# Turning float64 weight words into float32: four VectorE operations in place of three and one on GpSimd

## The chip, the cores and the metric

The kernel runs on 1 core of one Trainium2 chip. The metric is the device time of one execution in microseconds, the median of several runs. A profile records one further execution; its own time is the span from its first to its last instruction.

## The reference

The inputs are q, k and v (8 batches, 8 heads, 576 positions, 64 per head) and three weight matrices. Keys and values are averaged over groups of 8 positions, which leaves 72 of each. Then comes softmax attention against the 72, and a gated layer on the result:

```
k_p = k.reshape(B, H, Sp, 8, D).mean(axis=3);  v_p likewise      # Sp = 72
scores = matmul(q, k_p^T) / sqrt(D);  attn = softmax(scores)
x = matmul(attn, v_p) as [4608, 512]
out = ((x @ w_a) * (x @ w_b)) @ w_out            # w_a, w_b [512, 1536], w_out [1536, 512]
```

The weights arrive as float64, since they are scaled by a float64 number. The kernel reads them as pairs of 32-bit words and turns each pair into one float32 on the chip. The host only changes the layout.

## The kernel before

**Split products.** Every operand of a TensorE product is split into a high part (a rounded copy, made by ScalarE) and a low part (the difference, made by `low_part`, L171), and three products are summed in place of one.

**Tiles and steps.** The 4608 rows are worked in 9 tiles of 512. A tile takes 12 steps, one for each 128 of the 1536 inner columns. A step makes `a` (L552 to L554, PSUM tile psa), copies it to SBUF (L557), makes `b` (psb), multiplies both (L530), splits the product (hh L533, hl L171), and adds the product of the step before with w_out to `acc` (L573 to L575). For each step `split_weight` splits a block of each of the three weight matrices again (L238 on ScalarE: jha, jhb, jho; L171 on GpSimd: jla, jlb, jlo).

**Attention.** The queries come in 40 chunks (`chunk`): their scores (psc, L392), the scores less their maximum (L376, L377), exp (L426), the sum (z, L428 to L430), the division (s, L432), the split (pr, rem), the transposition (ptr L477, p L478) and the product with the values (po, L510 to L513, then xh and xl). Chunks of the first tile are done before the first step; those of a later tile run among the steps of the tile before it. `load_keys` and `load_values` average the keys and values (kp, vp, vwide, vdiag).

**Conversion.** `convert_weights(name, j, first)` is a generator for each of the matrices a, b and o. For each of 12 blocks of 128 x 512 it loads 1024 words per partition into its part of the tile `words` (one buffer for each matrix, L201), makes `low` (the low word by 2 to the power of -29, L211) and `mag` (the absolute value of the high word read as float32, L212) on ScalarE, then works on VectorE (L213, L216, L222) and ends with an addition on GpSimd (L226). Each converted block stays in SBUF for all 9 tiles, so the 36 conversions are done once, in the early part of the run.

**Order.** The order of each engine's instructions is written out by the program (`manual_schedule`). Each piece of work is a generator of class `Chains`; `yield n` puts its next part n slots later, and six slots make a step. Within a slot the ranks are: products, splits, chunks, weights, keys. From the third block on, a conversion waits until the step two before its own has begun, plus 0, 2 or 4 slots for a, b and o. Each engine works through its own instructions strictly in that order, and so does the queue of the DMA issues on SP.

Of the kernel before, what the change touches and what calls it, by code (L numbers as in the profile page):

```python
# [9 lines left out]
F32 = mybir.dt.float32  # L10
# [3 lines left out]
AF = mybir.ActivationFunctionType  # L14
ALU = mybir.AluOpType
# [10 lines left out]
NF = DF // P  # L26
NK = DM // P
# the high word of float64 2**-126, read as float32
MIN_HIGH = 2.0**-15 * 1.125
SCALE = 1.0 / float(D) ** 0.5  # L30
# [10 lines left out]

# of the pooled keys the first KM are multiplied with the values head pair by head pair, the KR
# that remain for four heads at a time: (hi, lo, hi) x 4 heads x KR rows
KM = D
KR = SP - KM
NR = 3 * 4 * KR
NG = H // 4
# a step of the inner loop takes this many slots of TensorE's time, a tile NF steps
SLOTS = 6
TILE_SLOTS = SLOTS * NF  # L50
# queries whose products with the values are made together: of the first two tiles, of the others
BLOCK, BLOCK_LATER = 256, 384
# tiles that hold something for a short time only
NTMP = 6
# chunks whose scores' three parts are summed in PSUM (the others' by VectorE)
SUMMED = 9
# steps by which the weights' conversion keeps ahead of the products, in the first tile
AHEAD = 2
# groups of TensorE's work in a slot in which the inner loop waits
GROUPS = 4  # L60
# slots: when a step's weights are split; between the parts of a chunk; what a chunk takes, and
# those of the second tile one after the other; how early a batch's keys and values come
SPLIT_A, SPLIT_B, SPLIT_O = 1, 4, 4
PROBS_GAP, VALUE_GAP = 2, 4
CHUNK, CHUNK_LATER, CHUNK_GAP = 34, 32, 10
KEYS_AHEAD, VALUES_AFTER = 18, 16
# the same before the first step: chunks one after the other, the values, the second batch's keys,
# the weights' loads and how much later their conversion begins
EARLY_GAP, VALUES_START, KEYS_START, WEIGHTS_START, CONVERT_AFTER = 1, 2, 4, 10, 5


class Chains:
    """Chains of work (generators), resumed slot by slot: a chain yields how many slots its next part
    comes later, or PE to get TensorE between two groups of the inner loop's products. done holds
    what has been issued."""

    PE = "PE"
# [36 lines left out]
def attn_moe_kernel(ctx: ExitStack, tc: tile.TileContext, q, k, v, vr, wa, wb, wo, out):  # L114
    nc = tc.nc
# [4 lines left out]
    PE = Chains.PE  # L120
    mark, wait, done = chains.mark, chains.wait, chains.done
    PRODUCTS, SPLITS, CHUNKS, WEIGHTS, KEYS = ((x, 0) for x in range(5))

    def tmp(name, dtype=F32):
        return sb.tile([P, 512], dtype, tag="tmp", name=name, bufs=NTMP)
# [5 lines left out]
    w_dram = {"a": wa, "b": wb, "o": wo}  # L131
    # pooled keys, heads in pairs on the diagonal: [(h%2, d), h//2, hi/lo, h%2, key]
    kdiag = [const.tile([P, NK, 2, 2, SP], F32R, name=f"kdiag{i}") for i in range(2)]
    # pooled values, heads in pairs on the diagonal: [(h%2, key), h//2, hi/lo, (h%2, d)]
    vdiag = [const.tile([P, NK, 2, P], F32R, name=f"vdiag{i}") for i in range(2)]
    # row (part, h%4, key) belongs to which of four heads
    mask = const.tile([P, 4], F32, name="mask")
    # where the weights' bits arrive: later the place of the blocks' transposed probabilities
    work = sb.tile([P, 2 * NK * BLOCK_LATER], I32, tag="work", name="words", bufs=1)
# [4 lines left out]
    early = sum(t == 0 for t in tile_of)  # L144
    # chunks of a batch and a tile whose products with the values are made together
    blocks, start = [], 0

    def cut(chunks, limit):
        """the cheapest blocks: a product takes its columns' time, or that of its weights' load"""
        best = None  # L150
        for x in range(1, len(chunks) + 1):
            total = sum(flat[c][2] for c in chunks[:x])
            if total > limit:
                break
            cost, rest = cut(chunks[x:], limit) if x < len(chunks) else (0, [])
            cost += max(total, 2 * P)
            if best is None or cost < best[0]:
                best = cost, [chunks[:x]] + rest
        return best
# [8 lines left out]
    vrems, parts, xtiles, turned, begun = {}, {}, {}, {}, []  # L168
# [3 lines left out]

    # the first batch's inputs wait where the last weights come later
    early_q = raw["a"][:, NF - early:, :].rearrange("p c (g s) -> p c g s", g=NK)
# [20 lines left out]
    def convert_weights(name, j, first):  # L195
        """float64 bits to the nearest float32: the sign and the exponent's top bit stay, 27 bits of
        the high word move up by three, what lies below float32's normal range becomes zero, and
        the low word rounds into the last three bits"""

        def load_words(f):  # L200
            nc.sync.dma_start(area[name], w_dram[name][:, f, :].bitcast(I32))  # L201

        load_words(0)
        yield first
        for f in range(NF):
            words = area[name].rearrange("p (c w) -> p c w", w=2)
            hi, lo = words[:, :, 1], words[:, :, 0]
            w = raw[name][:, f, :]
            wi = w.bitcast(I32)
            low, mag = tmp(f"wlow_{name}{f}", I32), tmp(f"wmag_{name}{f}")  # L210
            nc.scalar.activation(low, lo.bitcast(U32), AF.Copy, scale=2.0**-29)  # L211
            nc.scalar.activation(mag, hi.bitcast(F32), AF.Abs)  # L212
            nc.vector.tensor_scalar(  # L213
                out=wi, in0=hi, scalar1=0x07FFFFFF, scalar2=3, op0=ALU.bitwise_and, op1=ALU.logical_shift_left
            )
            nc.vector.scalar_tensor_tensor(  # L216
                out=wi, in0=hi, scalar=-(1 << 30), in1=wi, op0=ALU.bitwise_and, op1=ALU.bitwise_or
            )
            if f + 1 < NF:
                load_words(f + 1)  # L220
            yield 1
            nc.vector.scalar_tensor_tensor(  # L222
                out=w, in0=mag, scalar=MIN_HIGH, in1=w, op0=ALU.is_ge, op1=ALU.mult
            )
            yield 1
            nc.gpsimd.tensor_tensor(out=wi, in0=wi, in1=low, op=ALU.add)  # L226
            mark("weight", name, f)
            yield 2
            # not far ahead of the products, and not all three matrices at once
            while f + 1 >= AHEAD and (len(begun) <= f + 1 - AHEAD or chains.now < begun[f + 1 - AHEAD] + 2 * j):  # L230
                yield 1
# [52 lines left out]
    def load_values(b):  # L284
# [4 lines left out]
        for x0 in range(0, NK + NG, 2):  # L289
# [12 lines left out]
            for j in range(2):  # L302
                x, rows = x0 + j, P if x0 < NK else NR
                vv = vraw[j][:rows].rearrange("p (d j) -> p d j", j=POOL)
                if b == 0 and 0 < x < NK:
                    for n in (4, 2, 1):
                        to = vp[:rows, x].unsqueeze(2) if n == 1 else vv[:, :, :n]
# [5 lines left out]
        for e in range(2):  # L313
            r = slice(e * KM, e * KM + KM)
            nc.scalar.mul(vd[r, :, 0, r], vp[r, :NK], 1.0 / POOL)
        # each row's values at its head's place, zero at the others'
        wide = tmp(f"vwide_{b}").rearrange("p (r j e d) -> p r (j e) d", r=NG, j=2, e=2)
        for r in range(NG):
            nc.vector.scalar_tensor_tensor(
                out=wide[:NR, r],  # L320
                in0=vp[:NR, NK + r].unsqueeze(1).broadcast_to([NR, 4, D]),
                scalar=1.0 / POOL,
                in1=mask[:NR].unsqueeze(2).broadcast_to([NR, 4, D]),
                op0=ALU.mult,
                op1=ALU.mult,
# [5 lines left out]
        for e in range(2):  # L331
            r = slice(e * KM, e * KM + KM)
            nc.vector.scalar_tensor_tensor(
                out=vd[r, :, 1, r],
                in0=vp[r, :NK],
                scalar=1.0 / POOL,
                in1=vd[r, :, 0, r].bitcast(F32),
                op0=ALU.mult,
                op1=ALU.subtract,
# [8 lines left out]
    def chunk(i):  # L348
        b, o, n = flat[i]
        t, col = divmod(b * S + o, NT)  # L350
        first = i < early
# [14 lines left out]

        # scores less their maximum
        kd = kdiag[b % 2]
        s = sb.tile([P, H, SP], F32, tag="s", name=f"s_{i}")
        m = sb.tile([P, H], F32, tag="m", name=f"m_{i}")  # L370
# [52 lines left out]

        # probabilities
        yield 1
# [9 lines left out]
        yield 1  # L435
        # split, the keys that remain apart: [of four heads, (hi, lo, hi), h%4, key]
        yield from wait(("turned", i - 2))
# [11 lines left out]

        # transposed, and a block's products with the values  # L450
        j = block_of[i]
# [132 lines left out]
    def have(t):  # L584
        """all chunks of a tile are done"""
        return all(("value", block_of[i]) in done for i in range(len(flat)) if tile_of[i] == t)

    with tc.manual_schedule():
# [18 lines left out]

        # later chunks end in even steps, the first of them after what it takes to get there
        tail = [i for i in range(early, len(flat)) if tile_of[i] == 1]
# [76 lines left out]
```

## Time and profile before

| what | value |
| --- | --- |
| median of 3 runs | 1107.91 us (1107.82 to 1108.48) |
| span of the profiled execution | 1107.4 us |
| TensorE busy | 1038.7 us, 94% |
| VectorE (DVE) busy | 611.5 us, 55% |
| ScalarE (ACT) busy | 522.9 us, 47% |
| GpSimd (POOL) busy | 618.8 us, 56% |
| mean granted TensorE clock | 0.981 |

Busy time is the union of an engine's instructions. An instruction's recorded duration holds also the time in which it had been started and could not go on, so an operation of one shape can show quite different durations. The profile's 40 slices of 27.7 us show TensorE at 90% or more from the ninth slice on, and VectorE at 90% or more from the second to the eighth.

### The profile page before, as it was taken

Reading aid. Unit: us, or ns where it says so; the run is one execution under the profiler, and the core shown is the slowest. Engines: PE = TensorE matmul, PEld = TensorE weight load, DVE = VectorE, ACT = ScalarE, POOL = GpSimd, SP = SyncE. Lnnn points to the kernel's source line nnn. Section 1 sums busy time; section 2 is a strip of 40 time slices with the busy share of each in tenths; the row PEclk is TensorE's granted clock in tenths of the full one; section 3 lists DMA queues with packets and bytes.
Section 4 is the critical chain, followed back from the end, with each engine's and each line's share of the span. In section 5 each row is a group of like instructions: output and inputs, shape, how many; then the busy total and the mean of one; then the engine's idle time right before and its main releaser. Section 6 shows DMA issues by size and latency. Waiting matters only on the chain.

```text
span 1107.4 us, 13650 instructions
## 1 busy us (share of the span) xinstructions
PE 1038.7 (94%) x4964; PEld 861.7 (78%) x4964; DVE 611.5 (55%) x917; ACT 522.9 (47%) x1051; POOL 618.8 (56%) x501
## 2 busy tenths in 40 slices
PE   4378887899999999999999999999999999999998
PEld 4356665688887888888888888888888888888887
DVE  7999999863348333753367335654458343332212
ACT  3655555544445445544455445444445444443332
POOL 6557776655555555555555455554556455554442
PEclk9989888999999999999999999999999999999999
DMA  6454344120023000400021002200211020001001
GB/s 220 128 154 126 105 145 131 48 89 1 1 71 110 1 1 22 148 3 1 1 94 59 1 1 91 82 1 1 69 55 49 1 67 1 1 1 38 1 1 38
DMA packets 29874, 59.59 MB, mean 54 GB/s; under 512 B 7120, under 2 KB 7120, under 8 KB 29808
## 3 DMA queue, kind: packets, MB, share of 16 engines
q1 hardware_dynamic: 29808, 58.73, 16.9%
q8 instruction: 39, 0.64, 0.3%
q14 instruction: 27, 0.22, 0.1%
HBM read 49.28 MB, written 9.44 MB: 53 GB/s over the span
## 4 chain that ended last, share of the span: by engine, by line
PE 81%; DVE 14%; issue 2%; DMA 1%; ACT 1%; POOL 0%; SPq 0%; DVEq 0%; POOLq 0%; ACTq 0%
PE acc L573 9%; PE psa L552 8%; PE psb L552 8%; PE acc L575 8%; PE acc L574 8%; PE psa L554 8%; PE psa L553 8%; PE psb L554 8%; PE psb L553 8%; PE ptr L477 2%; PE psc L406 2%; DVE wo_raw L216 1%; DVE wo_raw L213 1%; DVE wa_raw L222 1%; DVE wb_raw L216 1%
## 5 line engine op out<-in xcount | busy, mean ns | idle before, releaser
L171 POOL TENSOR_TENSOR jlb<-wb_raw,jhb 128x512 fp32r<-128x512 f32 x108 | 142.9, 1323 | 220.9 <-ACT jhb L238 220.9
L530 DVE TENSOR_TENSOR h<-psb,h 128x512 f32<-128x512 f32 x108 | 74.5, 690 | 343.6 <-PE psb L554 340.4
L171 POOL TENSOR_TENSOR jla<-wa_raw,jha 128x512 fp32r<-128x512 f32 x108 | 143.9, 1332 | 143.0 <-ACT jha L238 117.5
L557 ACT COPY h<-psa 128x512 f32<-128x512 f32 x108 | 63.5, 588 | 244.1 <-PE psa L554 235.4
L573 PE MATMUL acc<-jho,hh 128*128 128x512 f32 x432 | 175.5, 406 | 0.0
L552 PE MATMUL psb<-xh,jhb 128*128 128x512 f32 x432 | 172.4, 399 | 2.1 <-DVE h L530 2.1
L552 PE MATMUL psa<-xh,jha 128*128 128x512 f32 x432 | 173.7, 402 | 0.0
L554 PE MATMUL psb<-xh,jlb 128*128 128x512 f32 x432 | 170.0, 393 | 2.4 <-POOL jlb L171 2.4
L553 PE MATMUL psa<-xl,jha 128*128 128x512 f32 x432 | 170.0, 393 | 1.0 <-DVE xl L171 1.0
L554 PE MATMUL psa<-xh,jla 128*128 128x512 f32 x432 | 170.0, 394 | 0.0
L575 PE MATMUL acc<-jho,hl 128*128 128x512 f32 x432 | 170.0, 393 | 0.0
L574 PE MATMUL acc<-jlo,hh 128*128 128x512 f32 x432 | 169.9, 393 | 0.0
L553 PE MATMUL psb<-xl,jhb 128*128 128x512 f32 x432 | 169.6, 393 | 0.0
L171 POOL TENSOR_TENSOR jlo<-wo_raw,jho 128x512 fp32r<-128x512 f32 x108 | 155.1, 1437 | 5.6 <-ACT jho L238 5.6
L171 DVE TENSOR_TENSOR hl<-h,hh 128x512 fp32r<-128x512 f32 x108 | 95.1, 880 | 20.7 <-ACT hh L533 20.6
L533 ACT CAST hh<-h 128x512 fp32r<-128x512 f32 x108 | 67.1, 622 | 72.6 <-DVE h L530 72.6
L554 PEld LDWEIGHTS psb<-xh,jlb 128*128 128x128 f32 x432 | 82.0, 190 | 20.8 <-POOL jlb L171 3.3
L575 PEld LDWEIGHTS acc<-jho,hl 128*128 128x128 f32 x432 | 81.9, 190 | 18.2 <-DVE hl L171 0.3
L554 PEld LDWEIGHTS psa<-xh,jla 128*128 128x128 f32 x432 | 82.1, 190 | 17.8
L552 PEld LDWEIGHTS psb<-xh,jhb 128*128 128x128 f32 x432 | 81.9, 190 | 17.8 <-issue 2.5
L553 PEld LDWEIGHTS psa<-xl,jha 128*128 128x128 f32 x432 | 82.4, 191 | 16.6 <-DVE xl L171 1.5
L552 PEld LDWEIGHTS psa<-xh,jha 128*128 128x128 f32 x432 | 82.2, 190 | 15.3
(92 smaller groups left out, 1776.3 us busy)
## 6 DMA issues: line engine op xcount, KB each, us to landing
out<-y SPq DMA_DIRECT2D x36, 256.0 KB, 2.2
kraw<-in_k SPq DMA_DIRECT2D x28, 288.0 KB, 3.9
vraw<-in_v SPq DMA_DIRECT2D x28, 256.0 KB, 3.1
qraw<-in_q SPq DMA_DIRECT2D x28, 256.0 KB, 3.8
words<-in_wa SPq DMA_DIRECT2D x12, 512.0 KB, 3.7
words<-in_wb SPq DMA_DIRECT2D x12, 512.0 KB, 3.7
words<-in_wo SPq DMA_DIRECT2D x12, 512.0 KB, 3.6
vraw<-in_vr SPq DMA_DIRECT2D x14, 192.0 KB, 2.6
```

The costliest lines, as they stand in the source:

```text
L171: eng.tensor_tensor(out=lo, in0=src, in1=hi.bitcast(F32), op=ALU.subtract)
L216: nc.vector.scalar_tensor_tensor(out=wi, in0=hi, scalar=-(1 << 30), in1=wi, op0=ALU.bitwise_and, op1=ALU.bitwise_or)
L406: nc.tensor.matmul(pt[:n, :2 * hk], qh[:, g, :n], kd[:, g].rearrange("p w e s -> p (w e s)"), start=True, stop=False)
L530: nc.vector.tensor_tensor(out=h, in0=pt, in1=h, op=ALU.mult)
L533: nc.scalar.copy(hh, h)
L552: nc.tensor.matmul(pt, wh[:, c], xh[:, kk], start=(kk == 0), stop=False)
L553: nc.tensor.matmul(pt, wh[:, c], xl[:, kk], start=False, stop=False)
L554: nc.tensor.matmul(pt, wl[:, c], xh[:, kk], start=False, stop=(kk == NK - 1))
L557: nc.scalar.copy(h, pt)
L573: nc.tensor.matmul(acc[c], hh[:, cs], wh, start=(f == 0), stop=False)
L574: nc.tensor.matmul(acc[c], hh[:, cs], wl, start=False, stop=False)
L575: nc.tensor.matmul(acc[c], hl[:, cs], wh, start=False, stop=(f == NF - 1))
```

## The change

`mag` is made ahead of `low`, both still on ScalarE. VectorE then raises `mag` to at least 2 to the power of -15 and scales it by 2 to the power of -16 (a float operation on one tensor), masks the result's bits and shifts them by three (in place, one tensor), and a slot later puts the sign from the high word to it (two tensors) and adds `low` (two tensors, on VectorE in place of GpSimd). The load of the next block's words is issued after the third operation, a slot later than before, and a block's conversion ends a slot earlier. Comments are taken out of the file too; line numbers stay close.

```
-            nc.scalar.activation(low, lo.bitcast(U32), AF.Copy, scale=2.0**-29)
             nc.scalar.activation(mag, hi.bitcast(F32), AF.Abs)
+            nc.scalar.activation(low, lo.bitcast(U32), AF.Copy, scale=2.0**-29)
+            nc.vector.tensor_scalar(out=w, in0=mag, scalar1=TINY, scalar2=2.0**-16, op0=ALU.max, op1=ALU.mult)
             nc.vector.tensor_scalar(
-                out=wi, in0=hi, scalar1=0x07FFFFFF, scalar2=3, op0=ALU.bitwise_and, op1=ALU.logical_shift_left
+                out=wi, in0=wi, scalar1=0x0FFFFFFF, scalar2=3, op0=ALU.bitwise_and, op1=ALU.logical_shift_left
             )
+            yield 1
             nc.vector.scalar_tensor_tensor(
-                out=wi, in0=hi, scalar=-(1 << 30), in1=wi, op0=ALU.bitwise_and, op1=ALU.bitwise_or
+                out=wi, in0=hi, scalar=-(1 << 31), in1=wi, op0=ALU.bitwise_and, op1=ALU.bitwise_or
             )
             if f + 1 < NF:
                 load_words(f + 1)
-            yield 1
-            nc.vector.scalar_tensor_tensor(
-                out=w, in0=mag, scalar=MIN_HIGH, in1=w, op0=ALU.is_ge, op1=ALU.mult
-            )
-            yield 1
-            nc.gpsimd.tensor_tensor(out=wi, in0=wi, in1=low, op=ALU.add)
+            nc.vector.tensor_tensor(out=wi, in0=wi, in1=low, op=ALU.add)
             mark("weight", name, f)
             yield 2
```

## Rows read from the trace of the kernel before

**Rows 1.** The page's busy time, share of the span and instructions, by engine.
```profile
PE 1038.7 (94%) x4964; PEld 861.7 (78%) x4964; DVE 611.5 (55%) x917; ACT 522.9 (47%) x1051; POOL 618.8 (56%) x501
```

**Rows 2.** Busy time by stretch: from:to, length, five engines, TensorE clock, DMA share, GB/s.
```profile
34.00:222.00 188.00, 142.40 (x633) 113.67 (x634) 180.24 (x220) 102.96 (x206) 127.30 (x93) 0.89 0.40 121
222.00:277.00 55.00, 55.00 (x271) 46.17 (x270) 26.82 (x42) 25.72 (x51) 31.64 (x25) 1.00 0.14 45
```

**Rows 3.** VectorE's waits, 34 to 222 us: in total, times, longest.
```profile
DVE vp L310 <- DMA vraw<-in_v: 2.4, 1, 2.4
DVE vp L310 <- DMA vraw<-in_vr: 0.9, 1, 0.9
DVE wa_raw L222 <- DVE wa_raw L216: 0.5, 1, 0.5
```

**Rows 4.** Single lines, L213, L216, L222, L226: count, ns min/median/max, first and last start.
```profile
L213 DVE TENSOR_SCALAR wb_raw<-words x12: 411/604/1487, 38.7 to 199.5; 128x512 int32<-128x512 int32 x12
...
L216 DVE SCALAR_TENSOR_TENSOR wa_raw<-words,wa_raw x12: 691/1657/3975, 35.7 to 194.4; 128x512 int32<-128x512 int32 x12
...
L222 DVE SCALAR_TENSOR_TENSOR wo_raw<-wmag_o,wo_raw x12: 630/692/1758, 48.0 to 204.9; 128x512 f32<-128x512 f32 x12
...
L226 POOL TENSOR_TENSOR wo_raw<-wo_raw,wlow_o x12: 1258/1648/1712, 48.7 to 206.5; 128x512 int32<-128x512 int32 x12
```

**Rows 5.** VectorE in order of time about 104.8 to 112 us: start, duration.
```profile
104.76 0.69 DVE L222 SCALAR_TENSOR_TENSOR wa_raw<-wmag_a,wa_raw 128x512 f32<-128x512 f32 x1
105.37 0.42 DVE L213 TENSOR_SCALAR wb_raw<-words 128x512 int32<-128x512 int32 x1
105.82 1.66 DVE L216 SCALAR_TENSOR_TENSOR wb_raw<-words,wb_raw 128x512 int32<-128x512 int32 x1
...
108.86 0.44 DVE L376 TENSOR_REDUCE m<-psc 64x4 f32<-64x288 f32 x1
109.33 0.45 DVE L377 TENSOR_TENSOR s<-psc,m 64x288 f32<-64x288 f32 x1
109.71 0.67 DVE L530 TENSOR_TENSOR h<-psb,h 128x512 f32<-128x512 f32 x1
110.31 0.41 DVE L213 TENSOR_SCALAR wo_raw<-words 128x512 int32<-128x512 int32 x1
```

**Rows 6.** GpSimd in order of time over the same stretch.
```profile
105.53 1.41 POOL L226 TENSOR_TENSOR wa_raw<-wa_raw,wlow_a 128x512 int32<-128x512 int32 x1 [1.42 <-DVE wa_raw L222]
109.01 1.27 POOL L226 TENSOR_TENSOR wb_raw<-wb_raw,wlow_b 128x512 int32<-128x512 int32 x1 [2.08 <-DVE wb_raw L222]
```

**Rows 7.** VectorE in order of time: the first and last stretched instructions, and two adjacent.
```profile
37.02 1.12 DVE L222 SCALAR_TENSOR_TENSOR wa_raw<-wmag_a,wa_raw 128x512 f32<-128x512 f32 x1
...
199.94 0.69 DVE L216 SCALAR_TENSOR_TENSOR wb_raw<-words,wb_raw 128x512 int32<-128x512 int32 x1
200.74 0.69 DVE L222 SCALAR_TENSOR_TENSOR wb_raw<-wmag_b,wb_raw 128x512 f32<-128x512 f32 x1
...
220.52 2.95 DVE L319 SCALAR_TENSOR_TENSOR vwide<-vp,mask 96x256 f32<-96x256 f32 x2
```

**Rows 8.** GpSimd's groups, 34 to 222 us: busy us, mean ns, idle before by releaser.
```profile
L171 POOL TENSOR_TENSOR jlo<-wo_raw,jho 128x512 fp32r<-128x512 f32 x12 | 19.3, 1609 | 0.0
L171 POOL TENSOR_TENSOR jlb<-wb_raw,jhb 128x512 fp32r<-128x512 f32 x13 | 18.9, 1456 | 6.5 <-ACT jhb L238 6.5
L171 POOL TENSOR_TENSOR jla<-wa_raw,jha 128x512 fp32r<-128x512 f32 x13 | 18.7, 1438 | 6.2 <-ACT jha L238 3.6 <-issue 2.0 <-POOL wo_raw L226 0.6
L226 POOL TENSOR_TENSOR wo_raw<-wo_raw,wlow_o 128x512 int32<-128x512 int32 x12 | 18.3, 1522 | 12.2 <-DVE wo_raw L222 12.2
L226 POOL TENSOR_TENSOR wa_raw<-wa_raw,wlow_a 128x512 int32<-128x512 int32 x12 | 16.4, 1365 | 10.1 <-DVE wa_raw L222 10.1
L226 POOL TENSOR_TENSOR wb_raw<-wb_raw,wlow_b 128x512 int32<-128x512 int32 x12 | 16.1, 1345 | 18.2 <-DVE wb_raw L222 16.3 <-PE ptr L477 1.9
```

**Rows 9.** ScalarE in order of time: two of the conversions' operations.
```profile
51.82 0.67 ACT L211 ACTIVATE wlow_o<-words 128x512 int32<-128x512 uint32 x1 [4.82 <-DMA words<-in_wo]
...
110.41 0.66 ACT L211 ACTIVATE wlow_o<-words 128x512 int32<-128x512 uint32 x1
110.98 0.66 ACT L212 ACTIVATE wmag_o<-words 128x512 f32<-128x512 f32 x1
```

More of the change, by code (lines that the diff above doesn't have):

```diff
@@ L27 @@
 NK = DM // P
-MIN_HIGH = 2.0**-15 * 1.125
+TINY = 2.0**-15
 SCALE = 1.0 / float(D) ** 0.5
@@ L210, in convert_weights @@
             low, mag = tmp(f"wlow_{name}{f}", I32), tmp(f"wmag_{name}{f}")
+            nc.scalar.activation(mag, hi.bitcast(F32), AF.Abs)
             nc.scalar.activation(low, lo.bitcast(U32), AF.Copy, scale=2.0**-29)
-            nc.scalar.activation(mag, hi.bitcast(F32), AF.Abs)
+            nc.vector.tensor_scalar(out=w, in0=mag, scalar1=TINY, scalar2=2.0**-16, op0=ALU.max, op1=ALU.mult)
             nc.vector.tensor_scalar(
-                out=wi, in0=hi, scalar1=0x07FFFFFF, scalar2=3, op0=ALU.bitwise_and, op1=ALU.logical_shift_left
+                out=wi, in0=wi, scalar1=0x0FFFFFFF, scalar2=3, op0=ALU.bitwise_and, op1=ALU.logical_shift_left
             )
+            yield 1
             nc.vector.scalar_tensor_tensor(
-                out=wi, in0=hi, scalar=-(1 << 30), in1=wi, op0=ALU.bitwise_and, op1=ALU.bitwise_or
+                out=wi, in0=hi, scalar=-(1 << 31), in1=wi, op0=ALU.bitwise_and, op1=ALU.bitwise_or
             )
```

## The prediction

> **What bounds the kernel now.** I read the shares of busy time first: TensorE 94%, every other engine about half [rows 1]. That says TensorE, for the whole run. The table by stretch says otherwise for the beginning: from 222 us on TensorE has no idle time and the full clock, but from 34 to 222 us it is busy 142.4 of 188 us while VectorE is busy 180.2 [rows 2]. All 36 conversions lie in that stretch [rows 4]. What TensorE has left at 222 us is fixed work at full speed, so a microsecond saved or lost before that point should move the end by about as much.
>
> VectorE's waits in the stretch name only 3.8 us [rows 3], so it runs its list without a pause. But is it working? The same conversion operation takes 0.69 us at best and 1.66 us in the median [rows 4]. The order of time shows why. At 105.53 us GpSimd begins its addition; VectorE's L216, started at 105.82, takes 1.66 us in place of 0.69 and ends when the addition has been over for some 0.5 us: 0.97 us lost to a 1.26 us GpSimd operation. At 109.01 the next addition runs beside L376, L377 and L530, and those keep 0.44, 0.45 and 0.67 us [rows 5, 6]. So the operations that read two SBUF tensors, and the one-tensor L213, exclude GpSimd's operations and are excluded by them; those that read PSUM are not.
>
> I took every VectorE instruction of the stretch against the shortest duration of its line and shape. 74 are over it by 0.1 us or more, the first L222 at 37.02 us, the last the second L319 in the row that begins at 220.52 [rows 7]; together they lose 68.5 us. Laid over the GpSimd operations that run in the lost time, 25.2 us fall on the 36 additions of L226 and 43.3 us on the other 56 operations (38 weight splits and 18 smaller ones of the chunks). Shortest durations give 36 x 1.258 = 45.3 us of GpSimd work for the additions and 63.3 us for the others (47.8 of it the splits) [rows 4, 8]. VectorE thus loses 0.56 us for each microsecond of additions, and 0.684 for each of the others.
>
> The Trainium skill ("SBUF — State Buffer", section "Who interferes with whom") says that a VectorE instruction with two SBUF inputs, or in a 2-port mode, and a GpSimd instruction block each other fully. On which forms are hit, the trace agrees (L216 1.66 us, L377 unchanged at 0.45); of the length it shows 0.97 us for a 1.26 us operation, and I use that.
>
> **The change part by part.**
>
> *The additions leave GpSimd:* -25.2 us of VectorE's lost time.
>
> *VectorE's own work.* Before: L213, L216, L222. After: two one-tensor operations, then two two-tensor ones. L222 and the addition have the same number of inputs and elements; no VectorE int32 addition is in the trace, so it is bounded by 0.63 (the shortest L222) and 0.69 us (the shortest L216), and I take 0.68. What is new is the second one-tensor operation, 0.41 us [rows 4]; the first is float rather than bitwise, taken as the same row. The spacing counts too: an operation that needs the one before it starts 0.03 us after its end (105.79 to 105.82) or, when it also waits for another engine, 0.11 after (200.63 to 200.74); one that needs neither starts 0.08 before that end (105.45 to 105.37) [rows 5, 7]. In the new order the sign operation and the addition are always neighbours (+0.10); before, L216 and L222 were neighbours 15 times in 36, with something between them 21 times, which averages to zero. So 0.41 - 0.00 + 0.10 = about 0.50 us for each conversion, 36 x 0.50 = +18.1 us. Bounds: 36 x 0.33 = 12 us with an independent instruction behind every part, 36 x (0.41 + 0.19) = 22 us if every L216 before had had an independent one behind it and now none has.
>
> The skill's page "VectorE: DVE Perf Modes" ("Rules for kernel authors") says that chained operations drain in any case and only their count matters; by that rule the term would be 36 x 0.41 = 14.8 us. The rows show a chained operation 0.11 to 0.19 us later than an unchained one, so I keep 18.1.
>
> *GpSimd's other 63.3 us stay* and meet more operations that can be excluded. In the new chain of four each gap lets a waiting split in. I raise their rate from 0.684 to 0.71: +1.6 us. Bounds: 0.55 (the rate of the additions, if the shorter GpSimd queue lets splits find free places) gives -8; 0.85 (nearly every split meets a chain; the single full meeting above is 0.97 / 1.26 = 0.77, and those behind an independent operation lose up to 1.14) gives +10.5.
>
> *VectorE waits for ScalarE.* The first operation now needs `mag`, where L213 needed only the loaded words. Moving `mag` ahead of `low` saves 0.57 us of that. With `mag` in `low`'s place I compared its end with the start of L213 for all 36: in 30 it is ready, by 0.15 to 5.6 us; in 6 it is late, by 3.6 us together (110.41 + 0.66 = 111.07 against 110.31: 0.76 [rows 5, 9]). Behind the waiting operation stand all products' and chunks' parts of VectorE. Some of this is time in which GpSimd holds VectorE up anyway: +2.0 us (0 to 6).
>
> *Loads.* The first load inside each chain is issued a slot later and its words are wanted a slot earlier. Before, ScalarE already stood 4.82 us for the second o block, until 51.82 us [rows 9], with the transposed probabilities of the first tile queued behind it. That arrival moves to about 52.3 to 53.3 us, and VectorE reaches its first use at about 53: +0.5 us (0 to 2). SP's other loads keep their places; later blocks have five of a step's six slots to arrive. ScalarE's own work is unchanged in amount, and 103 of 188 us busy [rows 2].
>
> *TensorE* waits less for GpSimd's splits, but that costs nothing while VectorE is last.
>
> Sum: -25.2 + 18.1 + 1.6 + 2.0 + 0.5 = -3.0 us. The profiled span is 1107.4, so 1104.4; the median of the runs is 0.5 above the span, so 1104.9 us.
>
> **The rivals.**
>
> *VectorE simply gets more work.* The remaining operations of GpSimd hit a VectorE that is busy with chains of four operations of the excluded kind; their rate goes to 0.85 and the ScalarE waits come in full: -25.2 + 18.1 + 10.5 + 3.6 + 0.5 = +7.5, 1115.4 us. For it: L216, the operation right behind a one-tensor one, is stretched most often (median 1.66 us [rows 4]). Against it: the rate has to rise by a quarter, while there are 36 operations fewer in GpSimd's queue. It decides from a rate of about 0.76 on. If, as the skill's page on SBUF says, each remaining operation cost its whole length (rate 1.0, +20 us), the time would be about 1123; L216's longest, 3.98 us under several GpSimd operations in a row, shows that this can happen, but no average of the trace is near it.
>
> *The splits get cheaper too.* With the rate at 0.55 and half the waits: -25.2 + 18.1 - 8.0 + 1.0 = -14.1, 1093.8 us. For it: after the additions of b the operations beside them were the chunks' PSUM readers, which lose nothing [rows 5, 6]; splits could take those places. Against: a split's place is set by ScalarE's copy, and that is where the conversions are.
>
> *The gain and the waits cancel.* All ScalarE waits and a full load wait: -25.2 + 18.1 + 1.6 + 3.6 + 2.0 = 0.1, 1108 us. For it: six waits are already visible by the old order alone.
>
> **How the numbers follow.** A measurement of this kernel can tell about 0.2%, 2.2 us, from no change. The forecast (between 2.2 and 9 us faster) has 0.36, the cheaper splits 0.14: faster 0.50. Cancelled: same 0.26. More work for VectorE: slower 0.24. Leaving about a tenth at either end: 1097 to 1115 us; the forecast's own range is 1099 to 1105.7.
>
> **What would show it.** In the changed profile: GpSimd 36 instructions fewer, and about 51 us less busy; VectorE 36 more (953). The addition at 0.6 to 0.7 us and both one-tensor operations at 0.41 when free; an addition over 1 us when free would break the second term. From 34 us to the point where TensorE is busy without a break, VectorE again without named waits over a few microseconds, and about 46 us of lost time in place of 68.5. The prediction is wrong if TensorE's unbroken stretch begins before 212 us or after 226 us, or if it begins as forecast and the end doesn't follow.

## The result, and the profile after

The changed kernel takes 1110.13 us (median of 15 runs, 1109.37 to 1112.34) against 1107.90 us before, taken beside it: ratio 1.0021, 95% interval 1.0014 to 1.0029. It is 2.2 us slower; 1104.9 us was forecast, 3 us faster. The time is inside the range of 1097 to 1115, the direction is wrong.

The page's line of busy time and the table by stretch, kernel after, answer to [rows 1, 2]:

```profile
PE 1036.8 (94%) x4964; PEld 861.5 (78%) x4964; DVE 601.3 (54%) x953; ACT 523.2 (47%) x1051; POOL 565.4 (51%) x465
```

```profile
34.00:222.00 188.00, 139.83 (x630) 113.01 (x630) 169.43 (x254) 102.78 (x205) 73.65 (x56) 0.84 0.39 121
222.00:277.00 55.00, 55.00 (x272) 46.10 (x271) 26.87 (x42) 25.58 (x51) 31.73 (x25) 1.00 0.14 45
```

GpSimd has 36 instructions fewer and in the stretch 53.7 us less to do. VectorE has 36 more and yet is busy for 10.8 us less. With such a line one would expect a gain. TensorE's mean granted clock in the stretch is 0.84 in place of 0.89, but that doesn't explain the time: VectorE's waits below name no TensorE operation, and of the runs further down the one with 0.86 (run 3) is 6.0 us faster than the change, one with 0.89 (run 6) 2.6 us slower. What VectorE waits for, 34 to 222 us (in total, times, longest), answers to [rows 3], where no ScalarE operation is named:

```profile
DVE wa_raw L214 <- ACT wmag_a L212: 2.8, 3, 1.3
DVE wo_raw L214 <- ACT wmag_o L212: 2.4, 3, 1.0
DVE vp L308 <- DMA vraw<-in_v: 2.1, 2, 1.9
DVE wb_raw L214 <- ACT wmag_b L212: 2.0, 2, 1.3
DVE xl L171 <- ACT xh L519: 1.5, 3, 0.7
```

7.2 us of waits for `mag`, eight times. The four operations by themselves (one row of each; count, ns min/median/max, first and last start) answer to [rows 4]:

```profile
L214 DVE TENSOR_SCALAR wb_raw<-wmag_b x12: 414/420/1411, 39.0 to 200.7; 128x512 f32<-128x512 f32 x12
...
L215 DVE TENSOR_SCALAR wb_raw<-wb_raw x12: 426/427/1376, 39.5 to 202.1; 128x512 int32<-128x512 int32 x12
...
L219 DVE SCALAR_TENSOR_TENSOR wa_raw<-words,wa_raw x12: 641/694/1810, 36.3 to 195.5; 128x512 int32<-128x512 int32 x12
...
L224 DVE CUSTOM_DVE_ANT_0 wa_raw<-wa_raw,wlow_a x12: 691/693/3084, 37.8 to 197.4; 128x1024 uint16<-128x1024 uint16 x12
L224 DVE CUSTOM_DVE_ANT_0 wb_raw<-wb_raw,wlow_b x12: 691/1476/1841, 44.0 to 203.4; 128x1024 uint16<-128x1024 uint16 x12
```

The sign operation now has a median of 0.694 us where L216 had 1.657. Over all three matrices 24 of the 36 L216 took over 1.3 us, of the sign operations 7; but 14 of the 36 additions do, 7 of them those of matrix b.

**A ledger of VectorE.** For each trace I went from the start of the first conversion operation to the end of the last. Each instruction's shortest duration among its kind goes into the first column, what it takes beyond that into the second; pauses up to 0.15 us less overlaps into the third, longer pauses into the fourth. All in us.

| trace | shortest | lost in operations | spacing | waits | sum | ends at | span |
| --- | --- | --- | --- | --- | --- | --- | --- |
| before, first trace | 108.4 | 66.6 | -5.3 | 1.4 | 171.1 | 206.5 | 1107.4 |
| before, second trace | 108.4 | 67.6 | -5.2 | 0.5 | 171.3 | 206.7 | 1106.3 |
| after | 123.1 | 41.0 | -1.0 | 9.1 | 172.1 | 207.1 | 1107.6 |
| addition on VectorE | 133.2 | 42.4 | -10.5 | 1.0 | 166.2 | 201.4 | 1103.5 |
| no addition | 108.6 | 38.1 | -4.7 | 3.8 | 145.8 | 181.5 | 1080.9 |
| no wait for mag | 123.2 | 41.3 | -1.0 | 3.5 | 166.9 | 202.6 | 1103.1 |
| low first | 123.1 | 41.6 | -3.8 | 13.9 | 174.8 | 209.4 | 1109.9 |
| load early | 123.1 | 38.9 | -2.5 | 10.6 | 170.1 | 206.2 | 1106.6 |
| ScalarE a slot ahead | 123.4 | 41.9 | 2.0 | 5.5 | 172.9 | 209.0 | 1109.4 |
| ahead and early | 124.1 | 41.4 | 1.5 | 5.5 | 172.4 | 207.8 | 1108.3 |
| spread | 123.8 | 44.5 | -5.1 | 3.6 | 166.6 | 202.0 | 1103.4 |
| spread, low first | 124.1 | 43.3 | -5.3 | 7.5 | 169.7 | 205.0 | 1106.4 |

The span is the end of the last conversion on VectorE plus 899 to 902 us in every row, while the ends lie 28 us apart: what moves the last conversion moves the end by as much, as the prediction read it. A single trace moves by a microsecond or so: the one of after is of a run at 1109.42 us, 0.7 below its median, the second of before of one at 1108.23, 0.4 above. That accounts for the ledger's showing 1 us of the 2.2.

### The profile page after: what moved, and what is told of

It is laid out like the page before. It is cut to its first block, busy times and chain, and to the rows that moved or that the text cites. A ratio compares the mean times of both kernels' runs of the same rounds, so it can differ in the third digit from the quotient of the medians.

```text
span 1107.6 us, 13659 instructions
## 1 busy us (share of the span) xinstructions
PE 1036.8 (94%) x4964; PEld 861.5 (78%) x4964; DVE 601.3 (54%) x953; ACT 523.2 (47%) x1051; POOL 565.4 (51%) x465
## 4 chain that ended last, share of the span: by engine, by line
PE 82%; DVE 13%; ACT 2%; DMA 1%; issue 1%; POOL 0%; SPq 0%; DVEq 0%; ACTq 0%
PE acc L571 9%; PE psa L550 8%; PE psb L550 8%; PE acc L573 8%; PE acc L572 8%; PE psa L552 8%; PE psa L551 8%; PE psb L551 8%; PE psb L552 8%; PE ptr L475 2%; PE psc L404 2%; DVE wb_raw L224 1%; DVE wa_raw L224 1%; DVE wo_raw L224 1%; DVE wb_raw L219 1%
## 5 line engine op out<-in xcount | busy, mean ns | idle before, releaser
L528 DVE TENSOR_TENSOR h<-psb,h 128x512 f32<-128x512 f32 x108 | 74.5, 690 | 344.1 <-PE psb L552 334.3
L171 POOL TENSOR_TENSOR jla<-wa_raw,jha 128x512 fp32r<-128x512 f32 x108 | 143.1, 1325 | 196.4 <-ACT jha L236 170.1
L550 PE MATMUL psb<-xh,jhb 128*128 128x512 f32 x432 | 172.9, 400 | 4.6 <-DVE h L528 4.6
L551 PEld LDWEIGHTS psb<-xl,jhb 128*128 128x128 f32 x432 | 82.2, 190 | 15.2
```

Source lines behind the costliest of these rows:

```text
L171: eng.tensor_tensor(out=lo, in0=src, in1=hi.bitcast(F32), op=ALU.subtract)
L528: nc.vector.tensor_tensor(out=h, in0=pt, in1=h, op=ALU.mult)
L550: nc.tensor.matmul(pt, wh[:, c], xh[:, kk], start=(kk == 0), stop=False)
L551: nc.tensor.matmul(pt, wh[:, c], xl[:, kk], start=False, stop=False)
```

## The experiments

The times of before beside these runs were 1107.80 to 1107.94 us. In the expectations W is the theory that VectorE's waits for ScalarE cost the time.

**1. What GpSimd's additions cost.** The kernel before, without them:

```
-            nc.gpsimd.tensor_tensor(out=wi, in0=wi, in1=low, op=ALU.add)
```

> The kernel before, without the GpSimd addition of the low word (36 instructions; the weights lose their last bits). It prices those instructions by themselves. If VectorE's lost time under them is what they cost: 25 us faster than before, about 1083 us. Rival (TensorE or the order of the chunks would have held the stage back anyway): under 12 us faster, 1096 us or more.

1082.86 us, ratio 0.9774 (0.9761 to 0.9788): 25 us faster. Before, none of VectorE's waits names GpSimd [rows 3], TensorE's name an addition once (4.3 us), and the chain that ended last in the kernel before gives it 0%, by engine:

```profile
PE 81%; DVE 14%; issue 2%; DMA 1%; ACT 1%; POOL 0%; SPq 0%; DVEq 0%; POOLq 0%; ACTq 0%
```

The additions cost 25 us all the same, through VectorE's durations (66.6 us lost in operations before, 38.1 here). The former L216 in this run (a median of 0.69 us, where [rows 4] have 1.66):

```profile
L216 DVE SCALAR_TENSOR_TENSOR wa_raw<-words,wa_raw x12: 691/692/2771, 36.1 to 171.1; 128x512 int32<-128x512 int32 x12
```

**2. The engine alone.** The kernel before, with the addition on VectorE and nothing else changed:

```
-            nc.gpsimd.tensor_tensor(out=wi, in0=wi, in1=low, op=ALU.add)
+            nc.vector.tensor_tensor(out=wi, in0=wi, in1=low, op=ALU.add)
```

> The kernel before, with nothing changed but the engine of the addition: VectorE in place of GpSimd. VectorE's operations are then L213, L216, L222 and the addition, none of which waits for ScalarE late. Sum of the terms: -25 us of lost time, 36 x 0.61 = +22 us of work, some 1 us more lost under the splits: about 1105.5 us, 2 us faster than before. Theory W: this, so faster than the changed kernel by 4 to 5 us. Rival V: 22 us of work on the last engine are not given back, 1110 us or more.

1105.06 us, ratio 0.9974 (0.9965 to 0.9983), 2.7 us faster than before and the fastest version that computes the whole reference. Rival V falls: the work is given back. VectorE's waits in it, 34 to 210 us, name no `mag`:

```profile
DVE vp L310 <- DMA vraw<-in_v: 2.1, 2, 1.9
DVE m L376 <- PE psc L392: 1.0, 1, 1.0
```

Its own work is 10 us longer than in the change (133.2 against 123.1). It wins by 8 us of waits and 9.5 us of spacing. Most of the spacing is the addition's: it has other work ahead of it and starts 0.08 us before the end of that 35 times in 36, while the change's starts 0.03 to 0.14 us after the sign operation (-2.8 against +4.4 us over all 36). So of the two things that the change does, the move of the addition gains 2.7 us and the rest loses about 5.

**3. The waits, taken away.** The changed kernel, first operation:

```
-            nc.vector.tensor_scalar(out=w, in0=mag, scalar1=TINY, ...)
+            nc.vector.tensor_scalar(out=w, in0=hi.bitcast(F32), scalar1=TINY, ...)
```

> The changed kernel, whose first VectorE operation reads the high words themselves in place of their absolute value (negative weights then become zero; ScalarE still makes the absolute value, and nobody reads it). Nothing is moved; only VectorE's wait for ScalarE is gone. Theory W (those waits are what the prediction left out): 6 us faster than the changed kernel, 1104 us; a wait of about 1 us each for the early words stays. Rival C (the time is conserved: VectorE meets other waits or GpSimd instead, as in the run with ScalarE a slot ahead): 1109 to 1110 us.

1104.13 us (ratio 0.9969, 0.9957 to 0.9980): 6.0 us faster than the change, as W said; C would have had 1109 or more. Shortest durations, lost time and spacing are those of the change (123.2, 41.3, -1.0), so the difference is the waits. What is left of them:

```profile
DVE xl L171 <- ACT xh L521: 2.4, 3, 1.0
DVE vp L310 <- DMA vraw<-in_v: 2.1, 2, 1.8
DVE wo_raw L214 <- DMA words<-in_wo: 0.5, 1, 0.5
DVE z L428 <- ACT s L426: 0.3, 1, 0.3
```

**4. The waits, made longer.** The changed kernel with `low` ahead of `mag` on ScalarE:

```
+            nc.scalar.activation(low, lo.bitcast(U32), AF.Copy, scale=2.0**-29)
             nc.scalar.activation(mag, hi.bitcast(F32), AF.Abs)
-            nc.scalar.activation(low, lo.bitcast(U32), AF.Copy, scale=2.0**-29)
```

> The changed kernel with the two ScalarE operations in the old order, low ahead of the absolute value, so that mag is ready 0.57 us later. Theory W: each of the 8 waits for mag grows by 0.57 us and some of the conversions that were just in time begin to wait: 5 to 7 us slower than the changed kernel, 1115 to 1117 us. Rival C: 1110 to 1112 us.

1112.98 us, ratio 1.0050 (1.0036 to 1.0063): 2.85 us slower than the change, between W and C. The waits did grow as W said, from 7.2 us in 8 to 12.4 in 12:

```profile
DVE wo_raw L214 <- ACT wmag_o L213: 4.6, 4, 1.6
DVE wa_raw L214 <- ACT wmag_a L213: 4.5, 4, 1.5
DVE wb_raw L214 <- ACT wmag_b L213: 3.3, 4, 1.8
```

But the ledger's spacing fell by 2.8 us. That is the addition's own wait: with `low` made first, VectorE has waited for it already when it waits for `mag`, and the addition needs no second wait. In the change 31 of the 36 additions have a wait instruction of their own and start 0.136 us or a little more after the sign operation's end, the other 5 start 0.035 us after it; with `low` first there is no such instruction, and all 36 start 0.035 us after. I had not counted that. The change's wait instructions:

```profile
L224 DVEq EVENT_SEMAPHORE  x31: 21/21/21, 37.7 to 206.3; - x31
```

**5. The early loads.** The changed kernel with the sign operation and the load in the first slot:

```
+            nc.vector.scalar_tensor_tensor(out=wi, in0=hi, scalar=-(1 << 31), ...)
+            if f + 1 < NF:
+                load_words(f + 1)
             yield 1
             nc.vector.tensor_tensor(out=wi, in0=wi, in1=low, op=ALU.add)
```

> The changed kernel, with the sign operation and the load of the next words back in the first slot, as before the change; the addition stays in the second slot. Theory W: only the early waits on loaded words go (2.4 us of the 8.8), the first step starts at 57.5 to 58 us in place of 60.1, 1107.5 to 1108.5 us. Rival V: the first step starts earlier but VectorE's list is as long, no change, 1110 us.

1107.96 us, ratio 1.0002 (0.9993 to 1.0011): 2.2 us better than the change, as W said, but not in the way that it said. ScalarE's waits for words shrink from three to one (its waits from 34 to 60 us, first in the change, then here):

```profile
ACT wmag_o L212 <- DMA words<-in_wo: 4.3, 1, 4.3
...
ACT wmag_b L212 <- DMA words<-in_wb: 2.3, 1, 2.3
...
ACT wmag_a L212 <- DMA words<-in_wa: 0.7, 1, 0.7
```

```profile
ACT wmag_o L212 <- DMA words<-in_wo: 4.6, 1, 4.6
```

The first step's first product starts at 58.2 us in place of 59.7. But then VectorE waits 4.2 us once for values (`vraw`), and the second step begins at 68.8 us in place of 65.2. VectorE's waits for `mag` fall from 7.2 to 5.6 us. The ledger has 2.1 us less lost time and 1.5 less spacing, with 1.5 more waits in all. So 2.2 us is the measured worth of the edit; that it is the loads alone isn't shown, since the addition was also freed from the sign operation.

**6. ScalarE a slot ahead.** The changed kernel, with the pause between the engines' parts:

```
             nc.scalar.activation(low, lo.bitcast(U32), AF.Copy, scale=2.0**-29)
+            yield 1
             nc.vector.tensor_scalar(out=w, in0=mag, scalar1=TINY, ...)
...
-            yield 1
             nc.vector.scalar_tensor_tensor(out=wi, in0=hi, scalar=-(1 << 31), ...)
```

> The changed kernel, with both ScalarE operations of a conversion a slot ahead of its four VectorE operations (which then stand in one slot, the second). VectorE's waits for mag among the steps (6.4 of the 8.8 us in the changed kernel's trace) should go; the loads stay as late as in the change. Theory W (the time went into VectorE's waits for ScalarE): 6 us faster than the changed kernel, about 1104 us, and VectorE's named waits for mag under 3 us. Rival V (VectorE's own added work is what costs; what it does not wait for ScalarE it will wait for GpSimd): 1109 to 1111 us, with 50 us of lost time in place of 44.

1112.77 us, ratio 1.0041 (1.0029 to 1.0054): slower still, a clear miss for W. (The 8.8 and 6.4 us in the expectation hold 1.5 us of waits for xh; for `mag` alone it is 7.2 us, 4.9 of them not for late words.) The waits for `mag` are gone to the last, but others have come or grown, the longest of them:

```profile
DVE xl L171 <- ACT xh L519: 2.3, 2, 1.3
DVE h L528 <- PE psb L552: 1.2, 1, 1.2
DVE z L426 <- ACT s L424: 1.1, 3, 0.8
```

The ledger says where the gain went: the waits fall by 3.6 us in sum, but four operations in one slot are neighbours, each waiting for the one before, and the spacing rises by 3.0; the first conversion begins 1.1 us later, and 0.9 more is lost in operations.

**7. Ahead and early.** The same, with each conversion begun a slot sooner and its successor a slot later:

```
-        yield first
+        yield first - 1
...
-            yield 2
+            yield 3
```

> The changed kernel with ScalarE's operations a slot ahead, each conversion begun a slot earlier and its successor a slot later, so that loads and VectorE's operations stand in the slots of the kernel before. The run with ScalarE ahead began its conversions 1.1 us later and loaded late; that should be gone. Theory W: 1104 us (waits for mag gone, loads in time). Rival C: four operations in one slot are chained without anything between them, which cost that run 3 us of spacing; 1108 to 1110 us.

1110.75 us, ratio 1.0027 (1.0017 to 1.0037), a little over the 1108 to 1110 of C. It is 2.0 us better than run 6: the first conversion begins 0.8 us sooner, and lost time and spacing are 0.5 lower each. The chain stays (spacing 1.5).

**8, 9. Spread over three slots.** ScalarE's operations, then three VectorE operations and the load, then the addition:

```
-        yield first
+        yield first - 1
...
             nc.scalar.activation(low, lo.bitcast(U32), AF.Copy, scale=2.0**-29)
+            yield 1
             nc.vector.tensor_scalar(out=w, in0=mag, scalar1=TINY, ...)
...
-            yield 1
             nc.vector.scalar_tensor_tensor(out=wi, in0=hi, scalar=-(1 << 31), ...)
             if f + 1 < NF:
                 load_words(f + 1)
+            yield 1
             nc.vector.tensor_tensor(out=wi, in0=wi, in1=low, op=ALU.add)
```

> The changed kernel over three slots: ScalarE's two operations, then the first three VectorE operations and the load, then the addition; the whole begins a slot earlier. It joins what the runs so far priced one by one: no waits for mag (6.0 us by the run that reads the high words directly), the load in time (2.2 us by the run with the load in the first slot), and the addition not chained to the sign operation (0.11 + 0.08 us, 36 times, less what already was free). Theory W: 1101 to 1103 us. Rival C (the whole arrangement of ScalarE a slot ahead is what costs, as in the two runs with it): 1108 us or more.

> The same with low made ahead of the absolute value, so that the addition waits for nothing that VectorE has not already waited for. In the run with low first and no slot ahead VectorE's short pauses fell from 7.4 to 4.3 us while its waits grew by 5; with ScalarE a slot ahead the waits should not grow. Theory W: 2 to 3 us faster than the run without it, 1099 to 1101 us. Rival C: the same as the run without it within 1 us.

1106.34 us (0.9984, 0.9975 to 0.9992) and, with `low` first, 1106.36 us (0.9983, 0.9974 to 0.9992). The spread version is 3.8 us better than the change and 1.6 better than before. It breaks the chain (spacing -5.1 against 1.5 in run 7) and has no wait for `mag`, yet stays 3 to 5 us short of the sum of the single prices: 44.5 us are lost in operations, 3.5 more than in the change, and 2.1 us of its 3.6 us of waits are for values. Moving `low` brought nothing (spacing -5.3 against -5.1), so W of the last expectation missed and its C came true: in both versions 30 of the 36 additions start before the operation ahead of them has ended, so there was little left to save. The two traces are of runs 1.2 us under and 1.9 us over their medians and can't be set against each other by a microsecond. Why the lost time grew is not settled.

**10. The kernel before again,** unchanged, for a second trace:

> The kernel before, unchanged, for a second trace. Its first trace spans 1107.4 us although the runs' median is 1107.9 and all later profiles span 1.8 us less than their own time; so that trace should be of a run some 1.3 us over the median. Expected: span 1106.0 to 1106.5 us, first step at 55 to 57 us, VectorE's lost time in the conversions 65 to 67 us.

```profile
core 0: 1106.3 us, clock 0.983
```

The run took 1108.23 us, 1.9 over its span; with the other traces here it is 1.8. The first trace's 1107.4 thus probably belongs to a run near 1109.2 us; its own time was not given with it.

## Why the prediction was wrong

**What bounds the kernel: right.** Span and the last conversion's end move together over 28 us. (By the page's slices VectorE stands at 90% or more from the second to the seventh, not in the eighth, which stands below that.) TensorE's last pause of over 0.3 us ends at 215.5 us before and at 215.6 after, within the 212 to 226 that the prediction asked for.

**GpSimd's additions, -25.2 us: right.** Taking them out gains 25 us (run 1). In the ledger the lost time falls from 66.6 to 41.0, for this term and that of the other splits together.

**VectorE's own work, +18.1 us: right.** The ledger has 123.1 - 108.4 = 14.7 us more in shortest durations and 4.3 in spacing, 19.0 together. By the rule of the Trainium skill ("VectorE: DVE Perf Modes", "Rules for kernel authors") only the count of operations matters; it gave 14.8. The spacing that it leaves out is measured here, and runs 6 to 9 with the same operations range over 7 us by it.

**The other splits, +1.6 us: too high.** By the forecast the ledger's lost time would be 66.6 - 25.2 + 1.6 = 43.0 us; it is 41.0, so the rate fell a little where it was raised. Neither the rival with the rate at 0.85 nor that at 0.55 came about. The prediction's picture of a single meeting was wrong, though. It set the loss of 0.97 us against the addition's whole 1.26 us. But that addition had been running for 0.29 us when L216 started at 105.82, and ended at 106.94; L216 ended at 107.48, some 0.55 us later [rows 5, 6]. So it is with all 24 stretched L216: each ends 0.55 us after a GpSimd operation does. That is a full block until the other's end, as the Trainium skill has it ("SBUF — State Buffer", "Who interferes with whom"). The rate stays well under 1 since an operation that comes late loses only what remains, and many meet none; if each of the 56 had cost its whole length it would have been 63 us.

**VectorE waits for ScalarE, +2.0 us: this step failed.** It measures 7.2 us in the trace, 6.0 us when taken away (run 3). The prediction laid the new operation onto the old trace, found `mag` late 6 times by 3.6 us together, and then took 2.0, since part of it might lie under GpSimd's operations. Here are the eight waits of the kernel after, each beside what the old trace had for the same block (from the end of the operation in `low`'s place to the start of L213), and what ScalarE had itself waited for last, ahead of that `mag`:

| block | by the old trace `mag` is | measured wait, us | ScalarE's wait ahead of it, us |
| --- | --- | --- | --- |
| b, eighth | 1.36 late | 1.30 | 1.18, VectorE's L375 |
| o, sixth | 0.77 late | 0.70 | 4.26, VectorE's L375 |
| o, eleventh | 0.76 late | 0.71 | 2.40, VectorE's L375 |
| a, tenth | 0.30 late | 0.70 | 3.09, VectorE's L375 |
| a, fourth | 0.76 early | 0.76 | 3.59, VectorE's L528 |
| b, eleventh | 0.16 early | 0.72 | 0.87, TensorE's psa |
| a, second | 4.03 early | 1.34 | 0.73, loaded words |
| o, second | 1.56 early | 1.02 | 4.25, loaded words |

Of the six that the prediction had found, the two shortest (0.27 and 0.14 us) are gone and the other four came in full: 3.4 us, where the old trace had 3.2. Nothing of these four was hidden under GpSimd's operations, so the first fault is the discount to 2.0. The second is that the old trace doesn't show the other four, 3.8 us: two are of words that came late, and at two VectorE came to the operation sooner against ScalarE than before. In five of the eight, 4.2 us, ScalarE's list had just waited for VectorE itself. ScalarE and VectorE in order of time, kernel after:

```profile
111.69 0.68 ACT L424 ACTIVATE s<-s 64x576 f32<-64x576 f32 x1 [4.26 <-DVE s L375]
112.28 0.64 ACT L212 ACTIVATE wmag_o<-words 128x512 f32<-128x512 f32 x1
```

```profile
111.21 0.45 DVE L375 TENSOR_TENSOR s<-psc,m 64x288 f32<-64x288 f32 x1
111.58 0.67 DVE L528 TENSOR_TENSOR h<-psb,h 128x512 f32<-128x512 f32 x1
112.95 0.43 DVE L214 TENSOR_SCALAR wo_raw<-wmag_o 128x512 f32<-128x512 f32 x1 [0.70 <-ACT wmag_o L212]
```

ScalarE stands for 4.26 us until VectorE's L375 lets its exp begin, and only then comes to `mag`, whose words had landed at 105.4 us. VectorE has one operation to do meanwhile, then waits 0.70 us. However fast VectorE gets there, exp and `mag` still follow L375. The old kernel had the same order of lists (its exp is shown here, what follows it in [rows 5, 9]), but its first operation needed only the words:

```profile
109.82 0.69 ACT L426 ACTIVATE s<-s 64x576 f32<-64x576 f32 x1 [5.46 <-DVE s L377]
```

The sum with 7.2 in place of 2.0 is -3.0 + 5.2 = +2.2, just what was measured, and that is luck. The 7.2 hold the late words, which the next term prices too, and the other terms were off as well. In the ledger lost time is -25.6 (forecast -23.6), own work +19.0 (+18.1), waits of all kinds +7.7 (+2.5): +1.1 us together, and the rest of the 2.2 is what single traces miss. The waits are the only one of the three that is off by enough to turn the sign.

**Loads, +0.5 us: too small.** Two of the eight waits (1.34 us at 41 us, 1.02 us at 54) are of words that came late, together 2.4. The edit that loads early is worth 2.2 us (run 5), but also frees the addition. These overlap with the 7.2 and are not added to them.

The rival nearest to what happened was "the gain and the waits cancel", which had the two waits at 3.6 and 2.0 us. The rival on the slower side put its price in the wrong place.

## What to carry to other kernels

An engine with next to no place in the chain of waits can still set the pace through another engine's durations: compare each operation with its shortest before trusting the shares of busy time. And when an operation gets a new input from another engine, don't ask only whether that input was ready in the old trace: ask what its producer's list waits for just ahead of it. If that is the consumer itself, as in five of the eight waits here, the wait is built in. And where the old trace shows such a wait, count it in full.

## What the runs showed of the hardware

A VectorE operation that GpSimd holds up ends a fixed time after GpSimd's operation has ended. Of the 74 stretched operations of the kernel before, 45, with all the stretched L216 and L222, end about 0.55 us after the end of a GpSimd operation, 25, with all the stretched L213, about 0.28 us after, and four of small shapes 0.03 to 0.17 us after. The loss shows in the duration of the VectorE operation, not as a wait.

The int32 addition on VectorE appears in the trace as a custom operation on 128 x 1024 uint16, where GpSimd's showed 128 x 512 int32; alone it takes 0.69 us, no more than a two-input operation on 512 elements (L216, 0.69), and it too is held up by GpSimd (up to 3.08 us, beside three operations in a row, the end again 0.55 us after the last).

A wait instruction of its own ahead of an operation that needs the one before it costs about 0.10 us: 0.136 in place of 0.035 us between the two, 31 times (run 4).
